# Spreading the block means of the values with GpSimd instead of with DMAs

## The chip, the cores and the metric

The kernel runs on one core of one Trainium2 chip. The metric is the device time of one execution in microseconds; a time shown for a kernel is the median of several executions. The core's engines are TensorE (PE in the profile, with PEld for its weight loads), VectorE (DVE), ScalarE (ACT), GpSimd (POOL) and SyncE (SP), which here does nothing but issue DMAs.

## The reference

Three stages follow one another. Attention over 2 batches, 8 heads, 768 positions and a head dimension of 64: each query sees the keys less than 16 positions away, and beside them 24 summary keys, one for each block of 32 positions. A summary key is the maximum over its block, and its value is the **mean** over its block:

```
k_sum = k.reshape(B, H, nb, block, D).max(axis=3)
v_sum = v.reshape(B, H, nb, block, D).mean(axis=3)
scores_s = scale * np.einsum('bhsd,bhnd->bhsn', q, k_sum) + np.log(block)
a = softmax(concatenate([masked scores_l, scores_s]))
out = np.matmul(a, concatenate([v, v_sum]))
```

Then a mixture of 8 experts (1536 tokens, each sent to its best expert, 512 to 1024 to 512), and a dense layer pair (512 to 2048 to 512) with the mish function between. The output is 1536 x 512 in float32.

## The kernel before

The attention stage works on 24 groups, numbered g. A group is one batch b, 128 queries (i) and four heads (hh says which four). Groups 0 to 5 are batch 0 with hh = 0, groups 6 to 11 batch 0 with hh = 1, and from 12 on the two halves of the heads of batch 1 alternate. The 128 queries are two windows of 64 (t = 2i and 2i + 1, twelve windows in all). For each window, the tile `vw[b]` holds 120 rows for the second matmul: 96 rows (partitions 0 to 95) of values around the window, loaded straight from the input by `load_vw`, and 24 rows (partitions 96 to 119) of block means. The block means are the same for all twelve windows, so `vw[b]` holds twelve copies of them.

The means come about like this. `load_vb` brings all values of four heads in, `v_sums` adds up 32 positions with a reduction on VectorE (L1148, two halves) and scales on GpSimd (L1149) into the tile `vm`. `store_means` then issues four DMAs from SP, one for each head (L1154), each of which writes the 24 x 64 means of its head to the twelve places of `vw[b]`.

The order of all work is written out by hand (`manual_schedule`): a loop over steps g (L1618 to L1684) calls the pieces, and tables say which piece goes in which step (`loads` L1393, `prep` L1409, `means_at` L1425). Each engine, and SP's queue of DMAs, takes its instructions strictly in this order; waits between engines are put in by the framework. In step g the program does, in this order: DMA issues (`do_load`), the score matmuls of group g + 2 and their row maxima (`scores`, L1172 on PE; `top`, L1178 on DVE), preparation of q and k (`pack` L1037 or L1052 into `hp`; `k_windows` L1103 and `k_maxima` L1097 on DVE or ACT; `q_chunk` L1124), the transposition of group g's weights (L1207 on PE, L1214 or L1217 into `aT`), the exponentials of group g + 2 (`exps`, L1186 on ACT), the row sums (L1194, L1195 on DVE) and the normalisation of group g + 2 (`normalize`, L1200, on GpSimd from group 2 on), the second matmul of group g - 1 (`values`, L1228, tile `pv`), its copy `xT` (L1240), the product with the gate weights (L1245, L1249), the choice of the expert (`choose`, L1260 to L1274 on DVE), and last `store_means` where `means_at` names the step. `store_means(0, 0)` stands ahead of the loop.

GpSimd's queue in this stage holds the normalisations, the packing of some q and k pieces, the scaling of the means, and in step 7 the tables of the gate (L1381 to L1390).

Of the kernel before, what the change touches and what calls it, by code (L numbers as in the profile page):

```python
# [9 lines left out]
F32 = mybir.dt.float32  # L10
# [5 lines left out]
ALU = mybir.AluOpType  # L16
# [5 lines left out]
B, H, S, D = 2, 8, 768, 64  # L22
N, DM, E, F, FF = 1536, 512, 8, 1024, 2048
BLK, WIN = 32, 16
NBLK = S // BLK
TQ = 64
NTQ = S // TQ
KW = TQ + 2 * WIN
KC = KW + NBLK
# [90 lines left out]
def attention_moe_mish_kernel(  # L120
# [16 lines left out]
    nc = tc.nc  # L137
    V, A, G, T = nc.vector, nc.scalar, nc.gpsimd, nc.tensor
# [875 lines left out]
    with ExitStack() as at:  # L1014
        first_p = ExitStack()
        soon = first_p.enter_context(tc.tile_pool(name="soon", bufs=2, side="right"))
# [14 lines left out]
        raw, packed, kt, kw, ks, vw, vb, vm, qt = {}, {}, {}, {}, {}, {}, {}, {}, {}  # L1031
# [111 lines left out]
        def v_sums(b, hh, half):  # L1143
# [4 lines left out]
            V.tensor_reduce(out=m, in_=t[:, :, half * 32:half * 32 + 32].rearrange("p t d -> p d t"), axis=AX.X, op=ALU.add)  # L1148
            G.tensor_scalar(out=m, in0=m, scalar1=1.0 / BLK, scalar2=0.0, op0=ALU.mult, op1=ALU.add)  # L1149

        def store_means(b, hh):
            m = vm.pop((b, hh))
            for h in range(4):
                nc.sync.dma_start(  # L1154
                    out=vw[b][KW:KC, :, 4 * hh + h, :],
                    in_=m[h * NBLK:(h + 1) * NBLK].unsqueeze(1).to_broadcast([NBLK, NTQ, D]),
                )

        st, xT, xr = {}, {}, {}

        def scores(g):
            b, i, hh = groups[g]
            ps = ps_h.tile([128, 4, 128], F32, tag="h", name="ps")
            qc = qt[b, hh, i // 2]
            for j in range(2):
                for n in range(2):
                    t = 2 * i + n
                    var = 0 if t == 0 else (2 if t == NTQ - 1 else 1)
                    o = ps[:, 2 * j + n, 0:KC]
                    mask = cb[0:TQ + 3, M_MASK + var * KC:M_MASK + (var + 1) * KC]  # L1170
                    T.matmul(o, cb[0:TQ + 3, M_E:M_E + 128], mask, start=True, stop=False)
                    T.matmul(o, qc[:, j, t % 4, :], kw[b, hh][:, j, t, :], start=False, stop=True)  # L1172
            st["s", g] = ps

        def top(g):
            ps = st["s", g]
            nm = thr.tile([128, 4], F32, tag="nm", name="nm")
            V.tensor_reduce(out=nm, in_=ps[:, :, 0:KC], axis=AX.X, op=ALU.max, negate=True)  # L1178
            st["nm", g] = nm
# [12 lines left out]
        def sums(g):  # L1192
            sm = st["a", g][1]
            V.tensor_scalar(out=sm, in0=sm, scalar1=1e-9, scalar2=None, op0=ALU.add)  # L1194
            V.reciprocal(out=sm, in_=sm)  # L1195

        def normalize(g, eng):
            a, sm = st.pop(("a", g))
            an = thr.tile([128, 4, KC], F32, tag="an", name="an")
            eng.tensor_tensor(out=an, in0=a, in1=sm.unsqueeze(2).to_broadcast([128, 4, KC]), op=ALU.mult)  # L1200
            st["an", g] = an

        def transpose_a(g):
            an = st.pop(("an", g))
            pa = ps_x.tile([128, 4, 128], F32, tag="pa", name="pa")
            for j in range(4):
                T.transpose(pa[0:KC, j, :], an[:, j], ident)  # L1207
            st["pa", g] = pa
# [162 lines left out]
        def small_loads():  # L1371
            nc.sync.dma_start(out=gm[:, :, 128:136], in_=w_gate.rearrange("(j p) e -> p j e", p=128))
            mb = one.tile([128, 2, E], F32, name="mb")
            nc.sync.dma_start(out=mb, in_=bass.AP(modality_bias.tensor, modality_bias.offset, [[0, 128], [E, 2], [1, E]]))
            mi = one.tile([128, NT, 2], I32, name="mi")
            nc.sync.dma_start(out=mi, in_=modality_id.bitcast(I32).rearrange("(i p t) -> p i t", p=128, t=2))
            return mb, mi
# [46 lines left out]
        }  # L1424
        means_at = {5: (0, 1), 9: (1, 0), 13: (1, 1)}  # L1425
        norm_by = "VVGGGGGGGGGGGGGGGGGGGGGG"
        xt_by = "AA AA AV AA AA AV AA AA AA AV AA AA AA AA AA AA AA AA AA AA AA VV AA AA".split()

# [19 lines left out]
        def after(i, n):  # L1448
            return step_of[i] + n

        def do_load(x):
            kind = x[0]
            if kind in "qk":
                load_qk(*x)
            elif kind == "vw":
                load_vw(x[1], x[2], 0, 4)
            elif kind == "wv":
                load_vw(x[1], x[2], 4, 8)
            elif kind == "v":
                load_vw(x[1], x[2], 0, 8)  # L1460
            elif kind == "vb":
                load_vb(x[1], x[2])
            elif kind == "newvw":
                new_vw(x[1])

        def do_prep(x):
            kind = x[0]
            if kind == "k":
                k_chunk(*x[1:4], x[5])
            elif kind == "kw":  # L1470
                k_maxima(*x[1:4])
                k_windows(*x[1:5])
                if x[3] == 2:
                    k_blocks(*x[1:3], x[4])
            elif kind == "q":
                q_chunk(*x[1:4], x[5])
            elif kind == "m1":
                v_sums(x[1], x[2], 0)
            elif kind == "m2":
                v_sums(x[1], x[2], 1)  # L1480
# [15 lines left out]
        def packs(g):  # L1496
            for x in prep.get(g, ()):
                if x[0] in "qk":
                    pack(*x[:5])
# [35 lines left out]
        exps(1)  # L1535
        k_windows(0, 0, 2, "A")
        store_means(0, 0)
        sums(1)
        normalize(1, V)
        mb_mi = small_loads()  # L1540

        def mixed(*parts):
# [75 lines left out]
        for g in range(NG + 2):  # L1618
            if g == 16:
                first_p.close()  # L1620
                split_p = ctx.enter_context(tc.tile_pool(name="split", bufs=2, side="right"))
                cv = ctx.enter_context(tc.tile_pool(name="cv", bufs=1, side="right"))
                moe = ExitStack()
                late_moe = ExitStack()
                rw = ctx.enter_context(tc.tile_pool(name="rw", bufs=3, side="right"))
                hp = ctx.enter_context(tc.tile_pool(name="hp", bufs=2, side="right"))
                xp = ctx.enter_context(tc.tile_pool(name="xp", bufs=1, side="right"))
                extra = moe.enter_context(tc.tile_pool(name="extra", bufs=1, side="right"))
            for x in loads.get(g + 1, ()):
                do_load(x)  # L1630
            packs(g + 1)
            if g + 2 < NG:
                scores(g + 2)
                top(g + 2)
            for x in prep.get(g - 1, ()):
                if x[0] not in "qk":
                    do_prep(x)
            for i0, n in batches:
                if after(i0 + n - 1, 3) == g < NG and i0 != NEARLY:
                    add_ids(i0, n)  # L1640
            for x in hooks.get((g, 0), ()):
                do_hook(x)
            for x in prep.get(g, ()):
                if x[0] in "qk":
                    do_prep(x)
            if g < NG:
                if early_values[g]:
                    values(g - 1)
                transpose_a(g)
                if early_exps[g]:  # L1650
                    exps(g + 2)
                store_aT(g)
            if g + 2 < NG and not early_exps[g]:
                exps(g + 2)
            if g + 2 < NG - 1 or g == NG - 2:
                mix(place(g))
            for x in hooks.get((g, 1), ()):
                do_hook(x)
            if g + 2 < NG:
                sums(g + 2)  # L1660
                normalize(g + 2, V if norm_by[g + 2] == "V" else G)
            if g == 7:
                gate_tables(*mb_mi)
            if g + 2 == NG - 1:
                mix(place(g))
            if 1 <= g <= NG:
                if g == NG or not early_values[g]:
                    values(g - 1)
                store_xT(g - 1)
            if g in gate_at:  # L1670
                gate_products(gate_at[g])
                gate_store(gate_at[g])
            for i0, n in batches:
                if step_of[i0 + n - 1] == g:
                    mix(choose(i0, n))
            if step_of[NT - 2] == g:
                mix(choose(NT - 2, 1))
            if step_of[NT - 2] + 1 == g:
                gate_exp(NT - 2, 1)
                mix(store_x(NT - 2, 1))  # L1680
            if g in means_at:
                store_means(*means_at[g])
            for x in hooks.get((g, 2), ()):
                do_hook(x)  # L1684
# [53 lines left out]
    for j in range(NU // 2):  # L1738
        a, b = 2 * j, 2 * j + 1
# [67 lines left out]
```

## Time and profile before

| | |
|---|---|
| time, median of 3 executions | 570.5 us (566.52 to 570.75) |
| profiled execution: its own time | 572.94 us |
| its span, first to last instruction | 570.9 us |
| mean granted TensorE clock | 0.981 |
| busy: PE, DVE, ACT, POOL | 531.7, 391.9, 387.0, 78.2 us |
| DMA packets, and those under 512 B | 75888, 28838 |
| DMAs that carry block means (L1154) | 16 of 72 KB |

The profiled execution is 2.44 us longer than the median of the timed ones; 2.04 us of it lie outside the span of its instructions. A line of the profile names a line of the kernel, an engine, an operation and its tiles (out<-in). Times in rows of a timeline are microseconds from the start of the span; the brackets at the end of a row say how long its engine was idle before it and what ended that.

### The profile page before, as it was taken

Reading aid. Unit: us, or ns where it says so; the run is one execution under the profiler, and the core shown is the slowest. Engines: PE = TensorE matmul, PEld = TensorE weight load, DVE = VectorE, ACT = ScalarE, POOL = GpSimd, SP = SyncE. Lnnn points to the kernel's source line nnn. Section 1 sums busy time; section 2 is a strip of 40 time slices with the busy share of each in tenths; the row PEclk is TensorE's granted clock in tenths of the full one; section 3 lists DMA queues with packets and bytes.
Section 4 is the critical chain, followed back from the end, with each engine's and each line's share of the span. In section 5 each row is a group of like instructions: output and inputs, shape, how many; then the busy total and the mean of one; then the engine's idle time right before and its main releaser. Section 6 shows DMA issues by size and latency. Waiting matters only on the chain.

```text
span 570.9 us, 9016 instructions
## 1 busy us (share of the span) xinstructions
PE 531.7 (93%) x3086; PEld 461.7 (81%) x3086; DVE 391.9 (69%) x909; ACT 387.0 (68%) x793; POOL 78.2 (14%) x126
## 2 busy tenths in 40 slices
PE   5888789878989999999999999999999999999995
PEld 4787689768979988899988888888888888888883
DVE  3897899865777767688879998645664565466442
ACT  4677776656454435465578999778877887887771
POOL 4155232221504100000000000004000002100003
PEclk9899899979999999999999999999999999999998
DMA  8999952083945957634332231001000000000001
GB/s 221 190 226 200 178 89 75 37 253 104 285 131 159 329 188 243 214 118 129 111 113 89 96 110 39 1 1 73 1 0 1 0 2 37 38 0 1 0 1 73
DMA packets 75888, 59.34 MB, mean 104 GB/s; under 512 B 28838, under 2 KB 66214, under 8 KB 75456
## 3 DMA queue, kind: packets, MB, share of 16 engines
q1 hardware_dynamic: 73200, 52.36, 34.7%
q0 software_dynamic: 2640, 6.38, 3.2%
q8 instruction: 25, 0.41, 0.3%
q14 instruction: 23, 0.19, 0.1%
HBM read 51.25 MB, written 6.29 MB: 101 GB/s over the span
## 4 chain that ended last, share of the span: by engine, by line
PE 51%; DVE 2%; ACT 2%; issue 1%; POOL 0%; POOLq 0%; DVEq 0%
PE ph L539 22%; PE o L1711 22%; PE ph L467 4%; PE o L485 3%; ACT L577 0%; DVE l L418 0%; DVE cin L520 0%; DVE xg L580 0%; POOL out_dram L1728 0%; DVE mol L491 0%; ACT cin L516 0%; ACT xg L577 0%; ACT xg L571 0%; POOLq L1803 0%; DVE cin L519 0%
## 5 line engine op out<-in xcount | busy, mean ns | idle before, releaser
L580 DVE TENSOR_TENSOR xg<-xg,ph 128x512 f32<-128x512 f32 x48 | 30.9, 684 | 94.5 <-ACT xg L577 94.5
L571 ACT ACTIVATE xg<-ph,cf 128x512 f32<-128x512 f32 x48 | 33.0, 687 | 38.7 <-PE ph L539 38.0
L467 PE MATMUL ph<-xh,h 128*128 128x290 f32 x160 | 50.2, 313 | 1.6 <-ACT h L417 1.6
L467 PE MATMUL ph<-xl,h 128*128 128x290 f32 x160 | 47.6, 297 | 0.4 <-DVE xl L451 0.4
L467 PE MATMUL ph<-xh,l 128*128 128x290 f32 x160 | 47.6, 298 | 0.3 <-DVE l L418 0.3
L1728 POOL DMA_INDIRECT out_dram<-ot,rows x9 | 10.8, 1203 | 245.6 <-DVE xh L561 87.2
L1186 ACT ACTIVATE a<-ps,nm 128x120 f32<-128x120 f32 x96 | 33.3, 362 | 16.1 <-DVE nm L1178 8.2
L1172 PE MATMUL ps<-kw,qb 128*128 128x120 f32 x192 | 37.9, 323 | 4.2 <-DVE qb L1124 4.2
L539 PE MATMUL ph<-moh,l 128*128 128x512 f32 x96 | 38.0, 396 | 0.0
L1711 PE MATMUL o<-h,gl 128*128 128x512 f32 x96 | 37.9, 395 | 0.0
L1711 PE MATMUL o<-h,gh 128*128 128x512 f32 x96 | 37.9, 395 | 0.0
L1711 PE MATMUL o<-l,gh 128*128 128x512 f32 x96 | 37.9, 395 | 0.0
L539 PE MATMUL ph<-moh,h 128*128 128x512 f32 x96 | 37.9, 394 | 0.0
L539 PE MATMUL ph<-mol,h 128*128 128x512 f32 x96 | 37.9, 394 | 0.0
L1172 PEld LDWEIGHTS ps<-kw,qb 128*128 128x128 f32 x192 | 32.4, 211 | 6.3 <-POOL kt L1079 3.0
L417 ACT CAST h<-cout 128x512 fp32r<-128x512 f32 x32 | 19.8, 619 | 21.0 <-PE o L485 16.5
L467 PEld LDWEIGHTS ph<-xh,h 128*128 128x128 f32 x160 | 30.4, 190 | 2.6 <-ACT h L417 1.8
L539 PE MATMUL ph<-moh,xh 128*128 128x512 f32 x96 | 31.9, 393 | 0.0
L539 PE MATMUL ph<-moh,xl 128*128 128x512 f32 x96 | 31.9, 393 | 0.0
L467 PEld LDWEIGHTS ph<-xl,h 128*128 128x128 f32 x160 | 30.4, 190 | 1.3 <-issue 0.7
L1228 PE MATMUL pv<-aT,vw 120*128 120x128 f32 x192 | 29.3, 300 | 2.3 <-DMA vw<-vm 1.4
L572 ACT ACTIVATE xg<-xg 128x512 f32<-128x512 f32 x48 | 30.4, 632 | 1.5
(332 smaller groups left out, 1593.5 us busy)
## 6 DMA issues: line engine op xcount, KB each, us to landing
r<-in_moe_w_dram SPq DMA_DIRECT2D x32, 256.0 KB
cr<-in_moe_w_in_dram SPq DMA_DIRECT2D x16, 512.0 KB
cr<-in_moe_w_out_dram SPq DMA_DIRECT2D x16, 512.0 KB
cout<-in_moe_w_dram SPq DMA_DIRECT2D x16, 256.0 KB
cin<-in_moe_w_dram SPq DMA_DIRECT2D x16, 256.0 KB
k<-in_k_dram SPq DMA_DIRECT2D x12, 256.0 KB
q<-in_q_dram SPq DMA_DIRECT2D x12, 256.0 KB
vb<-in_v_dram SPq DMA_DIRECT2D x4, 768.0 KB
```

The costliest lines, as they stand in the source:

```text
L417: A.copy(out=h, in_=r)
L467: T.matmul(ph[:, :W], a[:, kk, :], b[:, kk, :], start=n == 0, stop=n == 11)
L485: T.matmul(po[d][:, :W], a[:, d * 128:(d + 1) * 128], b, start=f == 0 and n == 0, stop=f == F // 128 - 1 and n == 2)
L539: ins.append(T.matmul(pt, a[:, kk, :], b[:, kk, c0:c0 + 512], start=n == 0, stop=n == 11))
L571: A.activation(out=t, in_=hps, func=AF.Sigmoid, bias=cf[:, C_B0:C_B0 + 1])
L572: A.activation(out=t, in_=t, func=AF.Arctan)
L580: V.tensor_tensor(out=t, in0=t, in1=ph.pop(u), op=ALU.mult)
L1172: T.matmul(o, qc[:, j, t % 4, :], kw[b, hh][:, j, t, :], start=False, stop=True)
L1186: A.activation(out=a[:, j], in_=ps[:, j, 0:KC], func=AF.Exp, bias=nm[:, j:j + 1], accum_out=sm[:, j:j + 1],)
L1228: T.matmul(pv[:, 2 * j + n, :], w, aT[0:KC, 2 * j + n, :])
L1711: T.matmul(acc[m], a[:, m * 128:(m + 1) * 128], b, start=f == 0 and n == 0, stop=f == NF2 - 1 and n == 2)
L1728: ins = G.indirect_dma_start(out=out[:, :], out_offset=bass.IndirectOffsetOnAxis(ap=at_rows, axis=0), in_=ot[:, :], in_offset=None,)
```

## The change

`store_means` no longer writes to the twelve places. Its four DMAs write the means once, to a new tile `vr` on the same partitions 96 to 119 (one buffer, used by all four pairs of batch and half). A new function, `spread_means`, has GpSimd copy a range of windows t0 to t1 from `vr` to `vw[b]`, as a multiplication by 1 over 24 partitions and (t1 - t0) x 256 elements. The copies are cut into nine instructions: one ahead of the loop, eight at the steps that the table `spread_at` names, each right behind the normalisation of that step on GpSimd. The means of batch 1, hh = 1 are stored in step 12 instead of 13.

```diff
+        vr = {}
         def store_means(b, hh):
             m = vm.pop((b, hh))
+            t = vr[b, hh] = soon.tile([128, 4, D], F32, tag="vr", name="vr", bufs=1)
             for h in range(4):
-                nc.sync.dma_start(
-                    out=vw[b][KW:KC, :, 4 * hh + h, :],
-                    in_=m[h * NBLK:(h + 1) * NBLK].unsqueeze(1).to_broadcast([NBLK, NTQ, D]),
-                )
+                nc.sync.dma_start(out=t[KW:KC, h, :], in_=m[h * NBLK:(h + 1) * NBLK])
+
+        def spread_means(b, hh, t0, t1):
+            G.tensor_scalar(
+                out=vw[b][KW:KC, t0:t1, 4 * hh:4 * hh + 4, :].rearrange("p t h d -> p t (h d)"),
+                in0=vr[b, hh][KW:KC].rearrange("p h d -> p (h d)").unsqueeze(1).to_broadcast([NBLK, t1 - t0, 4 * D]),
+                scalar1=1.0, scalar2=0.0, op0=ALU.mult, op1=ALU.add,
+            )
...
-        means_at = {5: (0, 1), 9: (1, 0), 13: (1, 1)}
+        means_at = {5: (0, 1), 9: (1, 0), 12: (1, 1)}
+        spread_at = {
+            0: (0, 0, 4, 8), 1: (0, 0, 8, 12), 6: (0, 1, 0, 6), 7: (0, 1, 6, 12),
+            10: (1, 0, 0, 4), 11: (1, 0, 4, 12), 13: (1, 1, 0, 4), 14: (1, 1, 4, 12),
+        }
...
         normalize(1, V)
+        spread_means(0, 0, 0, 4)
...
                 normalize(g + 2, V if norm_by[g + 2] == "V" else G)
+            if g in spread_at:
+                spread_means(*spread_at[g])
```

How the order on GpSimd moves around the start of the loop (- is before, + the change; L1200 and L1208 are the same normalisation, `an`; L1161 is the new copy, `vr` to `vw`; `hp` is the packing of a q and a k piece):

```order
 L1149 TENSOR_SCALAR vm<-vm 96x32 x2
+L1161 TENSOR_SCALAR vw<-vr 24x4x256
 L1078 MEMSET kt 128x2x16
 L1079 MEMSET kt 128x2x16
-L1200 TENSOR_TENSOR an<-a,sm 128x480 x2
+L1208 TENSOR_TENSOR an<-a,sm 128x480
+L1161 TENSOR_SCALAR vw<-vr 24x4x256
+L1208 TENSOR_TENSOR an<-a,sm 128x480
+L1161 TENSOR_SCALAR vw<-vr 24x4x256
 L1037 TENSOR_SCALAR hp<-q 128x512
 L1037 TENSOR_SCALAR hp<-k 128x512
```

Three copies of four windows each now stand there: one ahead of the normalisation of group 2, one behind it, one behind that of group 3 and ahead of the two packings.

The same on GpSimd around steps 12 to 14 (the `x8` are the normalisations of groups 14 to 21, `xg` the first gather of the experts' rows):

```order
 L1149 TENSOR_SCALAR vm<-vm 96x32
-L1200 TENSOR_TENSOR an<-a,sm 128x480 x8
+L1208 TENSOR_TENSOR an<-a,sm 128x480 x2
+L1161 TENSOR_SCALAR vw<-vr 24x4x256
+L1208 TENSOR_TENSOR an<-a,sm 128x480
+L1161 TENSOR_SCALAR vw<-vr 24x8x256
+L1208 TENSOR_TENSOR an<-a,sm 128x480 x5
 L440 DMA xg<-xs,ids_early 128x512 x2
```

Behind the normalisation of group 15 comes a copy of four windows, behind that of group 16 one of eight windows.

And on SP, at the last of the four stores of means (`q` is the last q piece of the stage, L1368 and L1376 the stores of the tokens):

```order
 L1135 DMA vw<-in_v_dram 96x8x64 x2
-L1042 DMA q<-in_q_dram 128x4x128
-L1154 DMA vw<-vm 24x12x64 x4
-L1368 DMA xs<-xr 128x512 x8
+L1158 DMA vr<-vm 24x64 x4
+L1042 DMA q<-in_q_dram 128x4x128
+L1376 DMA xs<-xr 128x512 x8
```

The four DMAs of the means now stand ahead of the load of the last q piece, and not behind it.

## Rows read from the trace of the kernel before

**Rows 1.** Busy time by stretch: busy us (x instructions) by engine, granted clock, DMA share, GB/s.

```profile
60.00:80.00 20.00, 15.84 (x125) 15.04 (x125) 17.83 (x37) 14.21 (x51) 5.80 (x9) 0.91 1.02 160
80.00:100.00 20.00, 18.27 (x164) 17.07 (x163) 18.22 (x74) 13.74 (x53) 4.19 (x4) 1.00 0.19 60
180.00:200.00 20.00, 20.00 (x150) 19.52 (x149) 15.03 (x39) 9.40 (x20) 6.63 (x7) 1.00 1.00 317
```

**Rows 2.** Timeline of DVE: start, us, instruction, idle before it (steps 5 to 8).

```profile
44.62 0.17 DVE L1194 TENSOR_SCALAR sm<-sm 128x4 f32<-128x4 f32 x1 [1.48 <-ACT a L1186]
...
51.28 0.17 DVE L1194 TENSOR_SCALAR sm<-sm 128x4 f32<-128x4 f32 x1 [0.60 <-ACT a L1186]
...
53.49 0.66 DVE L1178 TENSOR_REDUCE nm<-ps 128x4 f32<-128x480 f32 x1 [1.82 <-PE ps L1172]
```

**Rows 3.** Timeline of ACT in the same steps: packing of two k pieces.

```profile
41.90 0.62 ACT L1052 COPY hp<-k 128x512 f32<-128x512 f32 x1 [1.90 <-DMA k<-in_k_dram]
...
48.68 0.62 ACT L1052 COPY hp<-k 128x512 f32<-128x512 f32 x1 [0.63 <-DMA k<-in_k_dram]
```

**Rows 4.** Timeline of PE: the second matmuls of groups 6 and 13.

```profile
50.24 0.68 PE L1228 MATMUL pv<-aT,vw 120*128 120x128 f32 x4 [0.84 <-DMA vw<-vm]
51.46 0.68 PE L1228 MATMUL pv<-aT,vw 120*128 120x128 f32 x4 [0.53 <-DMA vw<-vm]
...
83.52 1.14 PE L1228 MATMUL pv<-aT,vw 120*128 120x128 f32 x8
```

**Rows 5.** Timeline of SP's queue: issue of DMAs.

```profile
18.70 3.47 SPq L1154 DMA_DIRECT2D vw<-vm  x4
...
23.34 0.43 SPq L1376 DMA_DIRECT2D mi<-in_moe_modality_id_dram  x1
...
72.57 1.42 SPq L1042 DMA_DIRECT2D q<-in_q_dram  x1
76.63 3.30 SPq L1154 DMA_DIRECT2D vw<-vm  x4
```

**Rows 6.** Groups of POOL, 0 to 130 us: busy us, mean ns, idle before.

```profile
L1037 POOL TENSOR_SCALAR hp<-k 128x512 f32<-128x512 f32 x2 | 1.2, 620 | 2.2 <-DVE nm L1178 2.2
L1381 POOL TENSOR_SCALAR gm<-cf 128x128 f32<-128x128 f32 x4 | 1.1, 302 | 0.0
```

**Rows 7.** Timeline of POOL: instructions beside which the new copies will stand.

```profile
26.15 0.99 POOL L1200 TENSOR_TENSOR an<-a,sm 128x480 f32<-128x480 f32 x1 [7.36 <-DVE sm L1195]
28.91 0.99 POOL L1200 TENSOR_TENSOR an<-a,sm 128x480 f32<-128x480 f32 x1 [1.77 <-DVE sm L1195]
...
48.45 0.99 POOL L1200 TENSOR_TENSOR an<-a,sm 128x480 f32<-128x480 f32 x1 [2.29 <-DVE sm L1195]
...
55.86 0.62 POOL L1037 TENSOR_SCALAR hp<-k 128x512 f32<-128x512 f32 x1
...
82.67 1.23 POOL L1200 TENSOR_TENSOR an<-a,sm 128x480 f32<-128x480 f32 x1 [3.45 <-PE pa L1207]
88.26 0.99 POOL L1200 TENSOR_TENSOR an<-a,sm 128x480 f32<-128x480 f32 x1 [4.37 <-DVE lg L1249]
```

**Rows 8.** Timeline of DVE: instructions with both ends in SBUF.

```profile
30.14 0.76 DVE L1103 COPY kw<-kt 128x768 f32<-128x768 f32 x1
...
56.50 0.55 DVE L1103 COPY kw<-kt 128x768 f32<-128x768 f32 x1
...
57.56 0.45 DVE L1103 COPY kw<-kt 128x576 f32<-128x576 f32 x1
...
82.63 1.54 DVE L1052 COPY hp<-q 128x512 f32<-128x512 f32 x2
...
88.62 0.66 DVE L1265 TENSOR_TENSOR lb<-lb,mx 128x16 f32<-128x16 f32 x1
89.31 0.17 DVE L1269 SCALAR_TENSOR_TENSOR eq<-lb,cf 128x16 f32<-128x16 f32 x1
...
131.82 0.17 DVE L1265 TENSOR_TENSOR lb<-lb,mx 128x8 f32<-128x8 f32 x1
```

## The prediction, made before the changed kernel was run

> **What bounds the kernel now.** I read the busy time by stretch first. From 180 us on TensorE is busy in all of 20.00 us [rows 1]: nothing this change touches is there, and whatever the attention stage gains or loses ahead of that moves the end by as much. In that stage TensorE has gaps (15.84 of 20 us from 60 on), the DMA engines are full until 80 us (share 1.02) and nearly idle afterwards (0.19), and VectorE is the fullest of the engines that are not TensorE: 17.83 and 18.22 of 20 us [rows 1]. So I went to VectorE's timeline and asked where it stands still. Between 28 and 68 us there are three gaps worth naming: 1.48, 0.60 and 1.82 us [rows 2]. The first two were ended by exponentials on ScalarE, and ScalarE had lost 1.90 and 0.63 us just before, waiting for k pieces to land [rows 3]. The third was ended by score matmuls that stood behind the second matmul of group 6, and that one had waited for the means themselves: its first four matmuls came at 50.24 (0.84 us idle), the others at 51.46 (0.53 us) [rows 4]. Hence all that DMA relief can give on VectorE, which I take as the path, is 1.48 + 0.60 + 1.82 = **3.9 us**. A q or k piece that lands earlier while VectorE is busy gives nothing.
>
> **The change, part by part.** Its own time is that of the profiled execution, 572.94 us, 2.44 above the median of 570.5; I make the sum of changes and apply it to both.
>
> *DMAs removed.* Each of the four stores of means now has 4 x 24 pieces of 256 bytes instead of 4 x 288. Issue on SP cost 3.47 us for four [rows 5]. What an issue with few pieces costs is not in the trace for this shape; bounds are 0.43 us, a small load [rows 5], and 0.87 (3.47 / 4, no gain). I take 0.43, since the number of pieces is what falls: 4 x 0.43 = 1.7 us, so every load behind the first store is issued 1.75 us earlier. The transfer falls too: two of the old ones kept the queue for 51.46 - 50.24 = 1.2 us [rows 4]. With 1.75 us the waits of 0.63 and, nearly, 1.90 for k pieces go [rows 3], and with them the gaps of 0.60 and 1.48 [rows 2]: **-2.1 us**, bounds 0 (buffers or the queue hold the pieces back anyway) and -2.1.
>
> *The third gap* does not go, because a wait takes its place. The means of group 6 are now there only when GpSimd has copied them, behind the normalisation that starts at 48.45 and takes 0.99 [rows 7]. The price of a copy: 128 columns take 302 ns and 512 take 620 [rows 6], 0.83 ns per column, so 1.04 us for four windows (1024 columns), 1.47 for six, 1.89 for eight. Lower bound 0.62, the 512-column row itself; upper bound twice the value, for a copy whose input repeats has no row. The copy of six windows ends at 48.45 + 0.99 + 1.47 = 50.9, then eight matmuls take 1.14 [rows 4]: 52.1, against 51.46 + 0.68 = 52.1 before. **0 us**, bounds -1.4 (the two waits) and +1.5. Its four DMAs must have landed by 49.4; the old first pair was through at 50.24 and had itself some 1.2 us of queue, so 49.0, less 1.75 of relief: in time.
>
> *Nine copies added on GpSimd*: 5 x 1.04 + 2 x 1.47 + 2 x 1.89 = 11.9 us, where it has 5.8 of 20 and 4.2 of 20 us busy [rows 1]. As GpSimd's own work that is free. What is not free is shown by two rows of VectorE: the subtraction in the choice of the expert took 0.66 us at 88.62 and ended at 89.28, when the normalisation on GpSimd that began at 88.26 had ended (89.25) [rows 7, 8]; at 131.82, half as wide and with GpSimd idle, it took 0.17 [rows 8]. So some VectorE instructions stand still until GpSimd's running one is done: this one with two inputs in SBUF, and copies out of SBUF too (0.76 against 0.55 us for the same kw copy [rows 8]). The Trainium skill, SBUF — State Buffer, Who interferes with whom, states this: the two share a port pair as an exclusive lock, held for the whole instruction, against VectorE's copies and tensor_scalars in two-port modes and its instructions with two SBUF inputs. The trace agrees (0.66 against 0.17 us).
>
> I went through the places.
> - Ahead of the loop: the first copy waits for DMAs that SP has issued by 18.70 + 1.7 = 20.4, and GpSimd idled 7.36 us before 26.15 [rows 5, 7]. Taken as 0, bounds 0 and 1.04, if it meets a VectorE copy.
> - Step 1: two copies sit around the normalisation of 28.91; the second runs from 29.9 to 30.9. VectorE's kw copy at 30.14 (0.76, alone 0.55) [rows 8] would end at 31.5 instead of 30.9: **+0.6 us**, bounds 0 and 1.2 (the packings behind it push on to the next kw copy). It eats into the gap of 1.48, but I count it in full since that gap is counted as gone.
> - Step 7: six windows ahead of the gate tables move the packing of 55.86 [rows 7] by 1.47 to 57.3, onto the kw copy of 57.56 [rows 8]: between 0 and 0.62, **+0.3**.
> - Step 10 and 11: VectorE's work there reads PSUM or reduces. 0. The scaling of the last means slides behind the copy of eight windows, up to 1.9 us, and SP now issues those means ahead of the last q piece. That load moves from 72.57 [rows 5] to about 76.63 + 1.9 + 1.7 = 80.2; VectorE packs it in the second half of the pair at 82.63 [rows 8], so about 3 us are left for it, with the DMA engines idle. 0, upper bound +2.
> - Step 13: the copy for group 13 starts behind the normalisation of 82.67 (1.23) and ends at 83.9 + 1.04 = 84.9; TensorE wanted it at 83.52 [rows 4, 7]. It waits 1.4 us, but VectorE is the later one in that step. 0, upper bound +1.4.
> - Step 14: eight windows behind the normalisation of 88.26: 89.3 to 91.2. VectorE's next instruction of the choice, at 89.31 with two SBUF inputs [rows 8], would wait for all of it, and row maxima, exponentials and the next choice stand behind it: **+1.9 us**, bounds 0 and 1.9.
>
> Sum: -2.1 + 0 + 0.6 + 0.3 + 1.9 = **+0.7 us**: 573.6 for the profiled execution, 571.2 by the median, and I say **571.2 us**: no change that could be measured. About 1% (5.7 us) is what a measurement of this kernel can tell from no change; its own three times lie 4.2 us apart.
>
> **The rivals.**
> *A. The DMAs were the path.* For it: DMA share of 1.02, and all three gaps end behind a landing [rows 1 to 4]. Against it: GpSimd's copy stands where the third wait was. If the copies meet no VectorE instruction that they can hold, and the third gap goes, -3.9 us: 566.6. If TensorE also no longer falls to the lower of its two levels, 1.2 GHz: the granted clock is 0.91 in 60 to 80 us [rows 1], that is 3.6 of 20 us at half rate, at most 1.8 us of matmul time; 564.8.
> *B. The lock decides, slower.* One mechanism: each copy holds VectorE for as long as it runs. My forecast lets 2.8 of the copies' 11.9 us fall on such VectorE instructions; from 2.1, a sixth, the change stops being a gain, and from 2.1 + 5.7 = 7.8, two thirds, it is over 1% slower. In full: 11.9 - 2.1 = +9.8, 580.3. For it: VectorE is over 89% busy where four of the nine copies run [rows 1]. Against it: many of its instructions there are reductions or read PSUM, and GpSimd waits too when VectorE comes first.
> *C. A late means.* Group 13 is the tightest: if the moved q load (+2) and the wait of 1.4 both land on the path, +3.4 more, 574.6. This is no case past 1% by itself; it widens the range upward.
>
> **How the numbers follow.** My forecast, with its losses near to its gains (569 to 574), 0.48; A 0.25; B 0.17; C 0.10. Faster by over 1% needs all of A and the clock: 0.09. Slower by over 1% needs most of B, or half of it with C: 0.16. Within: 0.75. For the range I cut a tenth at either side: down to A without the clock, 566.6, rounded to 566.3 for the spread of the runs; up to half of B's full price and C's wait of 1.4 on top (571.2 + 4.9 + 1.4 = 577.5), from which I take 577.
>
> **What would show it.** In the profile after: issues of L1158 near 0.43 us each; ScalarE's packing of k without a wait of 1.90; second matmuls of group 6 released by GpSimd at about 51; GpSimd's copies at 1.04, 1.47 and 1.89 us; and in step 14 an instruction of the choice (L1269 before) that takes near 2 us. TensorE's first expert matmul (L467) should start within 2 us of where it does before. I am wrong if copies take over 2 us for four windows, if VectorE's copies in steps 0 to 8 grow by more than 2 us together, or if a gap of VectorE or TensorE appears that a GpSimd copy ended, with more than 2 us.

## The result and the profile after

The changed kernel took **573.14 us** (median of 20 runs, 569.55 to 577.28), the kernel before 570.58 in as many runs beside it: ratio **1.0055**, 95% interval 1.0030 to 1.0081, some 3 us slower. In a second set of twelve runs it was 1.0027 (0.9990 to 1.0065), 1.5 us slower, with an interval that does not rule out no change. The forecast was 571.2, a sum of +0.7 us: within 1% as the result is, but 0.8 to 2.4 us too small, with several terms wrong.

The profiled executions hide the difference: their spans are 570.9 before and 570.8 after. By the step-15 row maxima the changed kernel is 3.03 us behind, and it makes that up outside the changed code: 0.8 in a shorter wait for the gather, 2.4 at 157 us, where in that one execution of before a weight landed late. First row: ScalarE's timeline there, second: TensorE's; the idle time stands in brackets with what ended it.

```profile
157.06 1.14 ACT L417 CAST h<-r 128x512 fp32r<-128x512 f32 x2 [3.93 <-DMA cout<-in_moe_w_dram]
158.25 0.40 PE L467 MATMUL ph<-xh,h 128*128 128x290 f32 x1 [1.58 <-ACT h L417]
```

Neither the second trace of before nor the two of the changed kernel (below) have that wait. So I compare stretches of the attention stage, not spans. Line numbers of after are higher by 8: row maxima L1186, packing of q and k L1037 and L1052 as before, the copies L1161, the stores L1158.

By stretch, the rows that answer to [rows 1]:

```profile
60.00:80.00 20.00, 18.27 (x139) 17.00 (x140) 18.89 (x36) 14.76 (x52) 11.09 (x15) 0.91 0.81 135
80.00:100.00 20.00, 16.25 (x145) 14.98 (x144) 16.92 (x66) 13.31 (x51) 6.17 (x5) 1.00 0.17 58
180.00:200.00 20.00, 20.00 (x149) 19.52 (x148) 15.08 (x39) 9.82 (x20) 6.57 (x7) 1.00 1.01 319
```

GpSimd (fifth column) has 11.09 us for 5.80, the DMA engines 0.81 for 1.02: work did move. TensorE and VectorE are busier than before from 60 to 80 us and idler from 80 to 100, which is where the time is lost.

VectorE's three gaps of [rows 2] after the change:

```profile
46.25 0.17 DVE L1202 TENSOR_SCALAR sm<-sm 128x4 f32<-128x4 f32 x1 [0.24 <-ACT a L1194]
...
52.72 0.17 DVE L1202 TENSOR_SCALAR sm<-sm 128x4 f32<-128x4 f32 x1 [0.41 <-ACT a L1194]
...
55.17 0.66 DVE L1186 TENSOR_REDUCE nm<-ps 128x4 f32<-128x480 f32 x1 [2.07 <-PE ps L1180]
```

The first is down from 1.48, the second from 0.60; the third stays (1.82). TensorE shows what took the DMA's place in it, and the wait of group 13, both as forecast [rows 4]:

```profile
52.66 1.16 PE L1236 MATMUL pv<-aT,vw 120*128 120x128 f32 x8 [1.54 <-POOL vw L1161]
...
85.60 1.16 PE L1236 MATMUL pv<-aT,vw 120*128 120x128 f32 x8 [1.42 <-POOL vw L1161]
```

SP's queue, for [rows 5], with the last store and the load that the change put behind it:

```profile
19.16 3.19 SPq L1158 DMA_DIRECT2D vr<-vm  x4
...
78.61 3.29 SPq L1158 DMA_DIRECT2D vr<-vm  x4
81.95 0.51 SPq L1042 DMA_DIRECT2D q<-in_q_dram  x1
```

Four issues still take 3.19 and 3.29 us, 0.8 each, although the pieces are a twelfth. The copies, on the other hand, cost what the columns said:

```profile
23.73 1.04 POOL L1161 TENSOR_SCALAR vw<-vr 24x1024 f32<-24x1024 f32 x1 [4.59 <-DMA vr<-vm]
...
51.14 1.47 POOL L1161 TENSOR_SCALAR vw<-vr 24x1536 f32<-24x1536 f32 x1
...
84.50 1.04 POOL L1161 TENSOR_SCALAR vw<-vr 24x1024 f32<-24x1024 f32 x1
90.98 1.93 POOL L1161 TENSOR_SCALAR vw<-vr 24x2048 f32<-24x2048 f32 x1
```

And VectorE, for [rows 8], in step 2 (beside the third copy, which GpSimd does at the end of step 1), from step 13 to step 15:

```profile
32.13 1.31 DVE L1103 COPY kw<-kt 128x768 f32<-128x768 f32 x1
...
82.84 0.18 DVE L1203 RECIPROCAL sm<-sm 128x4 f32<-128x4 f32 x1
...
85.07 0.76 DVE L1052 COPY hp<-q 128x512 f32<-128x512 f32 x1 [1.50 <-DMA q<-in_q_dram]
...
91.37 1.56 DVE L1282 TENSOR_TENSOR oh<-cf,cm 128x16 bf16<-128x16 f32 x1
92.85 0.64 DVE L1186 TENSOR_REDUCE nm<-ps 128x4 f32<-128x480 f32 x1
```

Two things are new. The second half of the pair of q packings, done in one go before, waits 1.50 us for its piece. And the last comparison of the choice (0.17 us before) takes 1.56 while the copy at 90.98 runs. The same two ends of this stretch in the kernel before:

```profile
82.32 0.18 DVE L1195 RECIPROCAL sm<-sm 128x4 f32<-128x4 f32 x1
...
89.82 0.65 DVE L1178 TENSOR_REDUCE nm<-ps 128x4 f32<-128x480 f32 x1
```

From the reciprocal of step 13 to the row maxima of step 15: **7.50 us before, 10.01 after**. This stretch is my measure for what follows, since it came out the same to 0.01 us in every trace in which the program of these steps was the same.

### The profile page after: what moved, and what is told of

Its sections match the earlier page's. It is cut to its first block, busy times and chain, and to the rows that moved or that the text cites. A ratio compares the mean times of both kernels' runs of the same rounds, so it can differ in the third digit from the quotient of the medians.

```text
span 570.8 us, 9022 instructions
## 1 busy us (share of the span) xinstructions
PE 533.1 (93%) x3086; PEld 462.9 (81%) x3086; DVE 393.7 (69%) x909; ACT 387.7 (68%) x793; POOL 90.5 (16%) x135
## 4 chain that ended last, share of the span: by engine, by line
PE 51%; DVE 2%; ACT 2%; issue 1%; POOL 0%; POOLq 0%; DVEq 0%
PE ph L539 22%; PE o L1726 22%; PE ph L467 4%; PE o L485 3%; ACT L577 0%; DVE l L418 0%; DVE cin L520 0%; DVE xg L580 0%; POOL out_dram L1743 0%; DVE mol L491 0%; ACT cin L516 0%; ACT xg L571 0%; ACT xg L577 0%; POOLq L1818 0%; DVE cin L519 0%
## 5 line engine op out<-in xcount | busy, mean ns | idle before, releaser
L1180 PE MATMUL ps<-kw,qb 128*128 128x120 f32 x192 | 39.1, 330 | 5.8 <-DVE qb L1124 4.2
L485 PE MATMUL o<-hh,h 128*128 128x290 f32 x96 | 29.5, 307 | 2.0 <-ACT xr L1259 2.0
```

The source lines that it names most:

```text
L485: T.matmul(po[d][:, :W], a[:, d * 128:(d + 1) * 128], b, start=f == 0 and n == 0, stop=f == F // 128 - 1 and n == 2)
```

## The experiments

All figures of a ratio are against the kernel before, with the 95% interval. My theory: the loss of 2.51 us has two causes, the late q piece and GpSimd's lock on VectorE; the rivals are that the lock alone does it, that TensorE's waits for the copies do it, or that the gain on the DMA side was missing.

**1. The last q piece first.** Changed kernel, with

```
-            14: [("q", 1, 1, 2)],        (loads)
+            if g == 12: do_load(("q", 1, 1, 2))
             if g in means_at: store_means(*means_at[g])
```

> Only SP's order is changed: the load of the last q piece, q(1,1,2), goes out at the end of step 12 ahead of the means of (1,1), not behind them. Changed kernel: VectorE waited 1.50 us for that piece (hp<-q at 85.07). If the order of the queue cost this time (late load): the wait of 1.50 is gone, the row maxima behind it come 1.1 us earlier against the start of step 13, and the time is about 0.8 to 1.1 us (0.15 to 0.2%) below the changed kernel's, ratio to before 1.0035 to 1.004. If only the lock of the GpSimd copies costs time: the wait is gone, but the copies of steps 13 and 14 (1.04 and 1.93 us) now meet VectorE the same way, the choice at step 14 still stands 1.56 us, and 1.0055 stays. If neither matters because the gather's wait further on absorbs it (3.2 us before, 2.4 after): the row maxima of step 13 are 1.1 us earlier, but the first expert matmul is not.

Measured: ratio 1.0013 (0.9979 to 1.0046). VectorE, steps 13 and 14:

```profile
82.89 1.54 DVE L1052 COPY hp<-q 128x512 f32<-128x512 f32 x2
...
90.05 1.74 DVE L1273 TENSOR_TENSOR lb<-lb,mx 128x16 f32<-128x16 f32 x1
...
92.24 0.17 DVE L1282 TENSOR_TENSOR oh<-cf,cm 128x16 bf16<-128x16 f32 x1
```

The wait for q is gone, yet the stretch takes 9.76 us. GpSimd's copy of eight windows now starts at 89.87 and holds the subtraction, 1.74 us for 0.66 [rows 8], where it had held the comparison; two other instructions with both inputs in SBUF lose 0.28 and 0.25. And VectorE now waits 0.54 us for TensorE, which had waited 1.47 us for the copy of group 13:

```profile
85.39 2.06 PE L1236 MATMUL pv<-aT,vw 120*128 120x128 f32 x8 [1.47 <-POOL vw L1161]
...
89.16 0.19 DVE L1257 TENSOR_REDUCE lg<-px 128x8 f32<-128x32 f32 x1 [0.54 <-PE px L1253]
```

Those matmuls took 2.06 us for 1.16, on the lower level of the clock (0.91 granted from 80 to 100 us, 1.00 in the first trace after). The copy alone doesn't make this gap: in experiment 10 TensorE waits 1.47 us for it too, its matmuls take 1.30, and VectorE has no gap there. Of the 2.26 us that stay above the 7.50 of before, 1.6 are the lock's and 0.6 this wait's. One cause removed gives 0.25 us, because the waits behind it take its place. The interval of the time is too wide to say more.

**2. Copies in pieces of two windows.** Changed kernel, `for t in range(t0, t1, 2)` around the copy.

> Each copy is cut into pieces of two windows (512 columns), 24 pieces where there were 9 copies; nothing else. By the row of 512 columns (620 ns) GpSimd needs 24 x 0.62 = 14.9 us where it needed 11.9. If a GpSimd instruction holds VectorE's copies and two-input instructions until it ends (lock per instruction): no VectorE instruction stands more than 0.62 us longer than alone, the choice's comparison at step 14 (1.56 us) takes at most 0.8, the kw copy of 1.31 at most 1.2; the choice is 0.8 to 1.4 us earlier; ratio to before 1.002 to 1.004. If VectorE is slowed by the total of GpSimd's traffic on the port and not by the length of one instruction: the loss stays, summed over more instructions, 1.0055 to 1.008. If GpSimd's copies are only a wait of TensorE (groups 6 and 13): each end comes 0.4 to 0.6 us later than that of the uncut copy, and the time rises by as much.

Measured: ratio 1.0037 (1.0010 to 1.0065). In steps 13 and 14:

```profile
85.14 0.87 DVE L1052 COPY hp<-q 128x512 f32<-128x512 f32 x1 [1.65 <-DMA q<-in_q_dram]
...
91.56 0.27 DVE L1283 TENSOR_TENSOR oh<-cf,cm 128x16 bf16<-128x16 f32 x1
```

The comparison stands 0.27 us, while the four pieces on GpSimd take 2.68 us from 91.17 on, more than the one long copy. So it is the length of the running instruction that VectorE waits for, not GpSimd's total. The stretch takes 9.00; the q piece is still late. The third gap fell too, from 2.07 to 0.93: group 6's matmuls wait for the pieces that they read, not for all six windows.

**3. Stores of 32 partitions.** Changed kernel, `out=t[KW:128, h, :], in_=m[h*24:h*24+32]`, the small tile eight partitions longer.

> Each DMA of the means moves 32 partitions where it moved 24 (the eight behind hold values that no matmul reads; a memset of GpSimd fills the last ones); pieces still 256 bytes, copies unchanged. My forecast took 0.43 us for an issue, from a load of 128 partitions; in the changed kernel four issues took 3.19 us, 0.80 each, and 0.87 with twelve times the pieces. If the price hangs on how the partitions fall on the queues (24 partitions do not spread over all 16 engines): about 0.43 to 0.5 us each, 1.2 to 1.5 us less per store, and the loads behind the first store 1.3 us earlier, so the k pieces' waits on ScalarE shrink by as much; ratio 1.003 to 1.005. If a DMA from SBUF to SBUF costs SP 0.8 us whatever its shape: 3.1 to 3.3 us for four, time unchanged, 1.0055.

Measured: ratio 1.0039 (1.0009 to 1.0069), and SP's queue:

```profile
18.68 2.49 SPq L1159 DMA_DIRECT2D vr<-vm  x4
44.33 3.22 SPq L1159 DMA_DIRECT2D vr<-vm  x4
62.80 3.88 SPq L1159 DMA_DIRECT2D vr<-vm  x4
77.44 2.83 SPq L1159 DMA_DIRECT2D vr<-vm  x4
```

On average 0.78 us an issue, as with 24 partitions (0.79), spread more. Neither the number of pieces nor these partitions set the price; the price of the small load (0.43) does not hold for a store from SBUF to SBUF. Why not stays open. Steps 13 and 14 take 10.01, as in the changed kernel.

**4. The first group by the old stores.** Changed kernel; (0,0) is stored as before, its three copies are left out.

> The group (0,0) goes the old way (four DMAs of 288 pieces into all twelve places), so the three copies ahead of the loop and in steps 0 and 1 are left out; the other three groups as in the changed kernel. If the copies' lock costs VectorE about 1 us in steps 1 to 3 (kw copies of 1.31, 0.86 and 1.08 us where before had 0.76, 0.45 and 0.65): these are back at 0.76, 0.45, 0.65, and the time falls by what is then not lost again. If the smaller transfers of this group are what removed the two gaps before 44.62 and 51.28 (1.48 and 0.60 us in before): both come back, and the time is that of the changed kernel or up to 0.5 us more. Copies alone: ratio 1.003 to 1.004; transfers alone: 1.007; both: 1.0045 to 1.006.

Measured: ratio 1.0023 (0.9995 to 1.0052), steps 13 and 14 at 10.01. The kw copy beside the third GpSimd copy is back at 0.76, so its 1.31 was that copy's doing; the third one, in step 3, took 1.77 without any of these copies (0.65 in the first trace of before, 1.22 in the second), beside a normalisation and a memset of GpSimd (33.99 and 34.91). And VectorE's first gap (1.48 in before) shrinks to 0.57 without the small stores:

```profile
42.57 0.62 ACT L1052 COPY hp<-k 128x512 f32<-128x512 f32 x1 [0.91 <-DMA k<-in_k_dram]
...
45.28 0.17 DVE L1212 TENSOR_SCALAR sm<-sm 128x4 f32<-128x4 f32 x1 [0.57 <-ACT a L1204]
```

No DMA work had been taken away when the piece came at 42.57: the first small stores of this kernel go out at 45.04. That made me ask for a second trace of before.

**5. The kernel before, again.**

> The kernel before, unchanged, for a second trace: what in its first one is chance. If the k piece that ScalarE waited 1.90 us for at 41.90 is late by the program (full DMA queues), the gap of 1.48 us on VectorE before 44.62 is there again; if it is the landing's luck, it is shorter or gone, as in the four variants so far (0.24 to 0.70 us), of which one has the old stores for the first group. The waits near 70 us (1.05) and for group 6 (1.82) are in order of the program and should stand. The wait of 1.58 us on TensorE at 158 and the stretches at the lower clock between 112 and 130 us need not.

Measured: ratio 0.9996 (0.9959 to 1.0033). Steps 13 and 14: 7.50 again. The k piece and the gap:

```profile
42.19 0.62 ACT L1052 COPY hp<-k 128x512 f32<-128x512 f32 x1 [1.32 <-DMA k<-in_k_dram]
...
44.90 0.17 DVE L1194 TENSOR_SCALAR sm<-sm 128x4 f32<-128x4 f32 x1 [0.98 <-ACT a L1186]
```

The gap is 0.98 where it was 1.48: VectorE came 0.8 us later, the piece at about the same time. Its span is 566.1 against 570.9, and the clock is a part of that: 0.8 us behind at the row maxima of step 15, it is 2.4 ahead at the experts' first second product (L485, 135.55 for 137.98), over a stretch in which the clock was higher; the other 2.4 us are the late weight at 157 us, which it doesn't have. By stretch, granted clock in the third column from the end, first this second execution, then the first:

```profile
100.00:120.00 20.00, 15.77 (x140) 14.41 (x138) 16.42 (x84) 13.49 (x58) 7.16 (x7) 1.00 0.27 85
120.00:140.00 20.00, 15.60 (x125) 14.40 (x126) 13.52 (x59) 12.84 (x30) 3.23 (x8) 1.00 0.64 196
```

```profile
100.00:120.00 20.00, 16.19 (x133) 14.98 (x132) 16.30 (x87) 13.89 (x59) 7.63 (x8) 0.91 0.31 96
120.00:140.00 20.00, 15.93 (x108) 14.36 (x108) 11.48 (x45) 11.16 (x26) 1.41 (x4) 0.83 0.50 159
```

The same program ran this stretch at 1.00 throughout in one execution and partly at the lower level, 1.2 GHz, in another.

**6. Both edits together** (1 and 2).

> The first two edits together: the last q piece is loaded ahead of the means of (1,1), and every copy is cut into pieces of two windows. If the late q piece and the lock of the long copy are the two causes of the loss in steps 13 and 14 (2.5 us between the row maxima of step 12 and of step 15 in the changed kernel, 2.3 with the q piece alone mended, 1.5 with the copies alone cut): both waits are gone and the loss there is under 0.6 us; the row maxima that stand at 89.82 in before come at 89.8 to 90.6; ratio 0.998 to 1.001. If there is a third cause (TensorE's wait of 1.4 us for GpSimd at group 13): 1 us or more stays, ratio 1.002 or above.

Measured: ratio 1.0025 (0.9996 to 1.0053); the stretch takes **7.95**, so 2.06 of the 2.51 us are gone, though the edits alone gave 0.25 and 1.01. VectorE packs both q halves in one go (83.90, 1.54), the subtraction takes 0.67, and 0.45 us stay. The two ends of the stretch:

```profile
83.59 0.18 DVE L1204 RECIPROCAL sm<-sm 128x4 f32<-128x4 f32 x1
...
91.54 0.64 DVE L1187 TENSOR_REDUCE nm<-ps 128x4 f32<-128x480 f32 x1
```

The time fell less than the trace says; its interval holds both.

This trace also settles what [rows 8] left open, where the subtraction of 0.17 us was half as wide as that of 0.66. Here one of full width began just before a normalisation of GpSimd, and the next instruction of the choice, with two inputs in SBUF too, ran beside it:

```profile
79.70 0.99 POOL L1209 TENSOR_TENSOR an<-a,sm 128x480 f32<-128x480 f32 x1
```

```profile
79.59 0.17 DVE L1274 TENSOR_TENSOR lb<-lb,mx 128x16 f32<-128x16 f32 x1
79.80 0.92 DVE L1278 SCALAR_TENSOR_TENSOR eq<-lb,cf 128x16 f32<-128x16 f32 x1
```

So the width was not the reason, and a normalisation holds VectorE as a copy does.

**7. Copies for two groups only.** (0,1) in pieces of two windows and (1,0) in pieces of four; (0,0) and (1,1) by the old stores at their old places.

> Copies only for the groups (0,1), in pieces of two windows, and (1,0), in pieces of four; (0,0) and (1,1) go by the old stores at their old places, so SP's order of the q pieces is that of before. If the change pays only where the DMA engines are full and VectorE not held (steps 5 to 11), and costs at the start (lock on the kw copies) and at the end (steps 13 and 14): the third gap (1.82 in before, 2.07 changed, 0.93 in pieces) is near 0.9, the one of 1.05 near 70 us is gone, and the row maxima at 89.82 in before come 1 to 2 us earlier; ratio 0.996 to 0.999, the fastest of all. If what came earlier in the variants was the landing of k pieces by chance: within 0.5 us of before, ratio 1.000.

Measured: ratio 0.9992 (0.9959 to 1.0025). Steps 13 and 14: 7.50. The third gap, and TensorE's wait for the copy behind it:

```profile
54.01 0.66 DVE L1198 TENSOR_REDUCE nm<-ps 128x4 f32<-128x480 f32 x1 [0.93 <-PE ps L1192]
```

```profile
51.51 1.16 PE L1248 MATMUL pv<-aT,vw 120*128 120x128 f32 x8 [0.68 <-POOL vw L1173]
```

The loss is gone, and so little is gained that it can't be told from before.

**8. No copies at all.** Changed kernel with q first, copies left out.

> Left out of the computation: the block means' share of the output (no copies on GpSimd, the matmuls of the values read 96 rows where they read 120); the stores of the means still run, into the small tile, and the last q piece goes ahead of the means of (1,1). This is what the change would give if its copies were free. My forecast: the DMA relief is worth 2.1 us and, without the copy that takes the DMA wait's place, another 1.8, so VectorE's row maxima at 89.82 in before come 3 to 3.9 us earlier and the ratio is 0.993 to 0.995. If the relief is not there, since SP's issue of a small store costs as much as that of a large one: only the third gap goes, 1 to 1.8 us earlier, ratio 0.997 to 0.998. Against the copies in pieces with q first, the difference is what the copies still cost.

Measured: the whole kernel's time says nothing (1026 us: with other gate products the experts get other numbers of rows). In the attention stage steps 13 and 14 take 7.50. From VectorE's last k packing ahead of the loop (22.85 in before) to the reciprocal of step 13 it takes 58.86 us; the kernel before took 59.47 and 61.04, the changed kernel 59.42 and, in its second trace, 59.02. By this one trace free copies would thus give 0.6 to 2.2 us there, not 3.9: the third gap went, and 1.30 us of it came back as a wait for exponentials in the next step.

**9. The changed kernel, again.**

> The changed kernel, unchanged, for a second trace and more times. If the two causes in steps 13 and 14 are of the program: VectorE waits 1.3 to 1.7 us for the last q piece again, and one instruction of the choice stands 1.4 to 1.8 us under the copy of eight windows; the row maxima of step 15 come 1.5 to 2.5 us later, against those of step 13 of the first q half, than in either trace of before. The gap before 44.62 is 0.2 to 0.7 us. The granted clock between 100 and 140 us may be 1.0 or lower; the span goes with it (566 to 575 us). Ratio 1.003 to 1.0075.

Measured: ratio 1.0027 (0.9990 to 1.0065); steps 13 and 14 at 10.00, for 10.01 in the first trace. The same two rows:

```profile
84.13 0.91 DVE L1052 COPY hp<-q 128x512 f32<-128x512 f32 x1 [1.35 <-DMA q<-in_q_dram]
...
90.58 1.55 DVE L1282 TENSOR_TENSOR oh<-cf,cm 128x16 bf16<-128x16 f32 x1
```

VectorE's first gap was 1.04, above the expected 0.2 to 0.7, with the k piece at 42.79 after a wait of 1.37: the small stores did not make it land earlier.

**10. The long copy by ScalarE.** q first, and at the end of step 14 `A.copy(out=vw[1][KW:KC, 4:12, 4:8, :], ...)` in place of GpSimd's copy of eight windows.

> The last q piece goes ahead of the means of (1,1), and the copy of eight windows of (1,1) is done by ScalarE at the end of step 14; the other copies stay on GpSimd. With q first and the copy on GpSimd, the subtraction of the choice stood 1.74 us at 90.05 (0.66 in before). If it is GpSimd's instruction that holds VectorE (a shared port): subtraction 0.67 or less, comparison 0.17 to 0.18, and the row maxima of step 15 come 1.7 to 2.3 us earlier than with q first alone, less what the longer ScalarE queue gives back (its copy of about 2 us stands ahead of the q scaling and of aT: 0 to 1.5 us). If any engine's copy of that size into SBUF disturbs VectorE's reads: 1.5 us or more stays on the choice. Ratio 1.000 to 1.002.

Measured: ratio 1.0043 (1.0011 to 1.0074). The copy on ScalarE, then VectorE:

```profile
91.17 1.90 ACT L1698 COPY vw<-vr 24x2048 f32<-24x2048 f32 x1
```

```profile
90.97 0.65 DVE L1273 TENSOR_TENSOR lb<-lb,mx 128x16 f32<-128x16 f32 x1
...
92.07 0.17 DVE L1282 TENSOR_TENSOR oh<-cf,cm 128x16 bf16<-128x16 f32 x1
...
93.75 1.30 DVE L1124 TENSOR_SCALAR qb<-ps 64x512 f32<-64x512 f32 x2 [0.84 <-ACT qb L1122]
```

The same copy of the same length runs beside the comparison, and that takes 0.17 us. So it is GpSimd that holds VectorE. The stretch takes 7.90, but ScalarE's own work comes later, and VectorE waits 0.84 us for it right behind: from the same reciprocal to the row maxima of step 16 it takes 12.47 us, 12.70 with q first alone, 10.43 in before. The time is paid on another engine; it lies above the range that I expected.

**11. Copies ahead of the normalisation in step 6.** Kernel 7, the three pieces ahead of `sums` and `normalize`.

> As the kernel with copies for two groups alone, but in step 6 the three pieces for (0,1) stand ahead of the normalisation, not behind it. If GpSimd's order is what group 6 waits for (TensorE 0.68 us for the copy, VectorE 0.93 for the score matmuls behind): the pieces end by 50, that gap shrinks to 0.25 and the row maxima of step 15 come 0.2 to 0.7 us earlier; ratio 0.997 to 0.999. If the means' DMAs land only at about 50 us: the normalisation now waits behind the copies, 1 to 2 us, and transposes of group 7 with it; slower by 0.5 to 1.5 us, ratio 1.000 to 1.002.

Measured: ratio 1.0006 (0.9970 to 1.0042). The pieces wait for the means:

```profile
49.06 1.99 POOL L1173 TENSOR_SCALAR vw<-vr 24x512 f32<-24x512 f32 x3 [2.13 <-DMA vr<-vm]
```

The third gap is gone, but the normalisation behind them starts at 51.14, a gap of 1.42 us opens at 62 us, and one at 67 us is 1.58 for 1.02 in kernel 7; from the last k packing ahead of the loop to the row maxima of step 15 it takes 67.28 us, for 67.31 in kernel 7. The wait moved, as the second theory has it, and cost nothing. No version beat the kernel before by more than can be measured.

## Why the prediction was nearly right, and where it was not

- **VectorE as the path, gaps as the most to be won:** held as a bound. The terms up to step 13 add up to -1.2 us, and no gain there is shown. From the last k packing to the reciprocal of step 13 it took 59.42 and 59.02 us, and 59.59 and 61.43 in experiments 1 and 10, which are the changed kernel up to there but for the place of the last q load; before took 59.47 and 61.04. The two means differ by 0.4, and traces of like kernels by 1.6 and 2.4. A gap before 70.52 (1.05 and 1.12 us in before), which I did not name, went in both traces of the changed kernel but stands at 1.12 in experiment 10; why was not tested.
- **Issue, 0.43 us each: wrong.** Measured 0.80. I took a load from DRAM as the nearest row; a store from SBUF to SBUF has its own price. Four issues were shorter by at most 0.28 us, not by 1.75, and SP stood at the q load behind them anyway (28.04, 2.97 us before; 28.32, 2.24 after): the k piece whose wait I meant to remove went out at 37.91, for 37.53 before.
- **DMA relief, -2.1: wrong.** Where ScalarE waited for that piece, it came at 41.90, 42.19, 42.57 and 42.68 with the old first store (before twice, experiments 4 and 11), and between 41.40 and 43.43 in seven traces with the small one. It did not land earlier. The gap of 1.48 is a cushion: whoever comes later finds it smaller. That also swallows the lock of step 1, which has the size I gave it (1.31 against 0.76, +0.55 for +0.6) and no price that shows: without it, experiment 4 took 59.52 us up to step 13, no less than the changed kernel. I had counted the gap as gone and the lock in full; both stand against the same landing.
- **Third gap, 0:** right, 2.07 for 1.82, a wait for the DMA replaced by one for GpSimd.
- **Step 7, +0.3:** nothing; the kw copies took 0.55 and 0.44 us. Steps 10 and 11: nothing, as said; the reductions of the values beside the two copies (71.90 and 74.91) took 1.92 and 1.93 us, for 1.90 and 1.93 in before.
- **The moved q load, "0, upper bound +2": the step that failed, +1.1.** I let it go out at 80.2, with 3 us to spare. It went out at 81.95, since the four stores ahead took 3.29 us and not 1.7: the wrong price of the issue again. It landed about 85.0, where VectorE wanted it 1.5 us earlier; the row maxima behind it came 1.1 us later, counted from the reciprocal of step 13. Experiments 1 and 6 show it.
- **Group 13, 1.4 us of TensorE off the path:** right (1.42). It is hidden in experiment 10 too, where VectorE is not late; only with the matmuls on the lower level of the clock did 0.54 us of it reach VectorE (experiment 1).
- **The lock in step 14, +1.9: right in kind, +1.39 in size** (1.56 less 0.17), on the comparison and not on the instruction that I named, since the copy began at 90.98, after that one had begun. This agrees with the Trainium skill, SBUF — State Buffer, Who interferes with whom, which has GpSimd and VectorE take turns on a shared port for whole instructions: 1.56 under a copy of 1.93 us, 0.27 under pieces, 0.17 beside ScalarE.
- **Rivals.** A falls with experiment 8: free copies would not give 3.9 us. B has the right mechanism at about a tenth of its price (1.39 of 11.9 us): of the nine copies, one cost VectorE time that was not given back. C was half right: the q load landed on the path, the wait of group 13 did not.

With what was measured, 0 up to step 13, +1.1 and +1.4 behind it, the sum is +2.5; the times say +3.1 (1.7 to 4.6) and +1.5 (-0.6 to 3.7), and both intervals hold it. That +0.7 came so near is in part luck: a gain of 2.1 that did not show and a loss of 1.1 that I had put at 0 stand against 1.4 of losses too many (0.6 in step 1, 0.3 in step 7, 0.5 in step 14).

## What to carry to other kernels

Price an operation from a row of the same kind, ends in the same memories; where there is none, follow each bound of the price to everything that stands behind it in the queue: here one wrong issue price hid a late load. A gap that ends at a landing is a cushion, and a gain or a loss ahead of it is not to be added to it. And GpSimd's work is not free where VectorE has to wait out one of its long instructions: cut it, or put it beside instructions that it does not hold, and look again after each other change, since the lock falls on whatever is there then.

## What had not been expected of the hardware

- The issue of a store from SBUF to SBUF cost SP 0.83 to 0.87 us with 288 pieces, 0.79 with 24 and 0.62 to 0.97 with 32, beside 0.43 for a small load of 128 partitions.
- TensorE's level between 100 and 140 us differs between executions of one program: 0.91 and 0.83 by stretch, or 1.00 and 1.00, with spans of 570.9 and 566.1 (2.4 us of this are the late weight). TensorE had stood still just as long before, 3.18 and 3.24 us for the first gather of the experts' rows; the clock fell behind this wait in one execution and stayed in the other. Over the others the spans went the same way: 567.7 to 568.3 where both stretches had 1.00 (experiments 1 to 3), 571.4 to 573.9 where the second had 0.74 (4, 6 and 10); in experiments 2 and 3 that wait for the gather was 0.2 us besides, for 2.4 in experiment 1. These differences are as large as what the change costs, and a single profiled span can't show the change.
